# The third batch's q turned by VectorE instead of TensorE, with the order's positions chosen anew, in a linear-attention and softplus kernel

## The chip, the cores and the metric

The kernel runs on one core of a Trainium2 chip. The time is the device time in microseconds of one execution. Before the change it is 912.41 us, the median of three runs (911.59 to 914.95).

A core has engines that each work through a queue of their own, in order: TensorE (PE, matmuls; its weight loads are shown apart as PEld), VectorE (DVE), ScalarE (ACT), GpSimd (POOL) and SyncE (SP), which here only issues transfers between DRAM and on-chip memory. Sixteen DMA engines carry the transfers. Engines wait for each other through semaphores.

## The reference

Shapes: q, k, v are 8 batches x 8 heads x 576 rows x 64; x becomes 4608 tokens x 512; w_in is 512 x 2048 and w_out 2048 x 512.

```python
kv  = np.einsum('bhsd,bhse->bhde', k, v)
out = np.einsum('bhsd,bhde->bhse', q, kv)
rms = np.sqrt(np.mean(out * out, axis=-1, keepdims=True) + 1e-06)
x   = (out / rms * g_norm)            # then (B,H,S,D) -> (B*S, H*D)
h   = x @ w_in
g   = np.maximum(h, 0.0) + np.log1p(np.exp(-np.abs(h)))
y   = g @ w_out
```

## The kernel before, in words

**Three factors.** Each fp32 operand of the two large products is split into three parts (`high`, `low`, `less`), so that `h = x @ w_in` takes 12 matmuls per step (L660) and each of the three token tiles of a step takes 3 matmuls of `g @ w_out` (L667).

**Blocks, chunks and steps.** Tokens are cut into 36 tiles of 128 rows; three tiles make a block (384 tokens, 12 blocks). The inner width of 2048 is cut into 16 chunks of 128. A step is one block with one chunk: 192 steps in all. They are ordered in three phases: phase 0 takes every block with its first 4 chunks (blocks 0 to 3) or 6 chunks (the rest), phases 1 and 2 the later chunks. Between the phases the partial sums of a block go to DRAM (`part`) and come back. A step runs L660 on TensorE, softplus (L682) and a first factor (L684) on ScalarE, the two other factors (L671, L675) on VectorE, and then nine L667 on TensorE.

**From q to x.** For each batch `b`, k and v are loaded and multiplied to `kv` (L502). For each tile `t`, `rows(t)` takes q, needs it turned (head dimension on the partitions), multiplies it with `kv` (L521, `out_rows`, into a half of `o_banks`), squares on ScalarE (L590), sums on VectorE (L525), takes the power -0.5 on GpSimd (L528, L529) and scales on VectorE (L533). Tiles 0 to 11 are then turned by TensorE (L539), copied by ScalarE (L599) and stored to DRAM (L600); later tiles are turned in blocks of 32 by VectorE (L616) and stored by four transfers (L620). Each block's x is read back (L638) and split by ScalarE and VectorE (L445, L448, L452); for block 0 and the first pass of block 1 it is split right from TensorE's turn. Tiles of 128 rows do not line up with batches of 576: tile 13 holds 64 rows of batch 2 and 64 of batch 3, and tile 22 and others mix two batches as well.

**Two ways to turn q.** In `rows`, the condition at L548 chooses.

- By tiles: two transfers per tile piece (L567, `halves`, runs of 64 numbers, 256 bytes), then four TensorE transposes (L577) into `tp` or a half of `o_banks`, then a ScalarE copy (L584) into the tile `qT`.
- By batches: `load_q(b)` issues eight transfers (L423) that bring a whole batch's q into the buffer `qa`, in blocks of 32 x 32 that are laid out so that VectorE's block transpose finishes the turn. A transfer has 1152 runs of 32 numbers (128 bytes). Each tile piece is then one VectorE transpose (L552), which writes `qT` directly. Before the change this is used for batches 3 to 7 (`b >= 3`).

There is one `qa` buffer. The first of the eight transfers of a batch takes it and so waits until VectorE has made the last transpose of the batch before. Batch 0's whole tiles use `qa` as well, loaded by tiles.

**What sets the order.** All work is declared as tasks with an engine, a cost in ns, predecessors, buffers from rings (`rings`: 13 of `m`, one `qa`, two of `o`, one `tp`, two of `raw` and so on) and a position. `Plan.order()` walks through them with these costs: on each engine it takes the task that could start first, or, among those within 150 ns of it, the one with the lowest position. Where TensorE would stand idle for 400 ns or more before step 6, it puts in a filler matmul (`warm`, L778). The result is a fixed order for each queue; on the chip every instruction waits for its operands, and nothing overtakes on its engine. SyncE's transfers are one such queue: a store that waits for its data holds the loads behind it.

**Positions.** `P0` (L190) holds 40 numbers: `CONVERT` and `FETCH` place the first eight weight loads and their conversions; `EARLY` places the tiles of x, k and v, q, the reading back of x and of the partial sums; `LATER` places the later weights. In `weight`, the raw words of w_in or w_out are converted on ScalarE and VectorE (L294 to L324) and split (`divide`, L356 to L378).

Of the kernel before, what the change touches and what calls it, by code (L numbers as in the profile page):

```python
# [40 lines left out]
class Plan:  # L41
# [15 lines left out]
    def slot(self, ring):  # L57
        return Slot(ring)

    def add(self, engine, ns, run, after=(), pos=0.0, take=(), give=(), size=0, behind=None, follows=None):  # L60
        t = Task(engine, ns, run, [a for a in after if a is not None], pos, list(take), list(give), size)
        for s in t.give:
            s.readers += 1
        self.tasks.append(t)
        t.follows = follows
        t.behind = behind
        return t
# [79 lines left out]
def kernel(  # L147
# [39 lines left out]
    PLACES = 8  # L187
    LAST = PHASES[-1]

    P0 = [-88.5, 0.8, -46.3, -8.2, -11.1, 2.0, -42.9, 2.7, -64.0, -43.8, -63.7, -16.7, -31.2, -9.7, 0.3,  # L190
          -4.7, 5.0, -33.5, 16.5, 10.5, 5.5, 8.5, -2.0, 2.5, 3.5, 26.0, -22.0, 10.0, 4.5, 41.0, 50.0,
          65.5, 54.5, 72.0, 91.5, 94.5, 114.5, 106.0, 109.5, 8.5]
    CONVERT, FETCH, EARLY, LATER = P0[:8], P0[8:16], P0[16:27], P0[27:]
    BY_PE = 12
    AT_ONCE = 2 * TB
# [29 lines left out]
    def new(s, shape, dtype=F32):  # L225
        if s.ring == "o":
            s.tile = o_banks[:, :, s.place]
            return s.tile
        pool = ps if s.ring in PS else sb
        s.tile = pool.tile(shape, dtype, tag=f"{s.ring}_{s.place}", name=f"{s.ring}_{s.place}")  # L230
        return s.tile

    def pairs(x, p):

        return x[:, 2 * p:2 * p + 2].rearrange("r h d -> r (h d)")


    def halves(src, e):

        return src[e * NP:(e + 1) * NP].rearrange("p s d -> s p d")  # L240
# [155 lines left out]
    def parts(t):  # L396

        b, s0 = divmod(t * P, S)
        if s0 + P <= S:
            return [(b, 0, P, s0)]  # L400
        return [(b, 0, S - s0, s0), (b + 1, S - s0, P - S + s0, 0)]
# [11 lines left out]
    def load_q(b):  # L413


        q_slots[b], q_loads[b] = slot("qa"), []
        pos = x_pos(first_tile[b] + 1) - EARLY[7]

        def run(a, p):
            if not (a or p):  # L420
                new(q_slots[b], [P, NP * S])
            e, c = divmod(a, 2)
            nc.sync.dma_start(  # L423
                out=q_slots[b].tile[BL * a:BL * (a + 1), p * S:(p + 2) * S].rearrange("j (i d) -> j i d", d=BL),
                in_=q[b, e * NP + p:e * NP + p + 2, :, BL * c:BL * (c + 1)].rearrange("p (i j) d -> j (p i) d", j=BL))

        for a in range(4):
            for p in range(0, NP, 2):
                q_loads[b].append(add("SP", 500, lambda a=a, p=p: run(a, p), (), pos + 0.1 * (2 * a + p // 2),
                                      [q_slots[b]] if not (a or p) else [], [], 1095, behind=int(pos) - 3,  # L430
                                      follows=q_loads[b][-1] if a or p else None))
# [76 lines left out]
    def rows(t):  # L508
# [32 lines left out]
        def part_of_qT(n, r0):  # L541
            if qT.tile is None:
                new(qT, [P, NP, P])
            return qT.tile[:, :, r0:r0 + n]

        turned = []
        for b, r0, n, s0 in parts(t):
            if b >= 3:  # L548
                if b not in q_slots:
                    load_q(b)  # L550
                turned.append(add(
                    "DVE", 690 if n == P else 420, lambda b=b, r0=r0, n=n, s0=s0: nc.vector.transpose(  # L552
                        out=part_of_qT(n, r0),
                        in_=q_slots[b].tile.rearrange("k (p s) -> k p s", p=NP)[:, :, s0:s0 + n]),
                    q_loads[b], pos - 1, [qT] if not r0 else [], [q_slots[b]], follows=turned[-1] if turned else None))
                continue

            if 0 not in q_slots:
                q_slots[0] = slot("qa")
            at_qa = n == P and b == 0  # L560
            q_s = q_slots[0] if at_qa else slot("m")

            def load(b=b, n=n, s0=s0, q_s=q_s, at_qa=at_qa):
                if q_s.tile is None:
                    new(q_s, [P, NP * S] if at_qa else [P, H, D])
                for e in range(2):
                    nc.sync.dma_start(out=natural(q_s, at_qa)[:n, e::2], in_=halves(q[b, :, s0:s0 + n], e))  # L567

            def natural(q_s, at_qa):
                if not at_qa:  # L570
                    return q_s.tile
                return q_s.tile[:, t * d_model:(t + 1) * d_model].rearrange("s (h d) -> s h d", d=D)

            def turn_q(n=n, q_s=q_s, at_qa=at_qa, tp=slot("tp" if t < AT_ONCE else "o")):
                y = new(tp, [P, NP, P])
                for p in range(NP):
                    nc.tensor.transpose(y[:, p, :n], pairs(natural(q_s, at_qa)[:n], p), ident[:n, :n])  # L577

            tp = turn_q.__defaults__[-1]
            ld = add("SP", 900, load, (), pos - EARLY[7], [q_s] if not at_qa or t == 0 else [], [], 1220 * n // P,  # L580
                     behind=int(pos) - 3, follows=first_load[0] if t and at_qa else None)
            first_load.append(ld)
            a = add("PE", 440, turn_q, [ld], pos - 1, [tp], [q_s])
            turned.append(add("ACT", 590, lambda n=n, r0=r0, tp=tp: nc.scalar.copy(part_of_qT(n, r0), tp.tile[:, :, :n]),  # L584
                              [a], pos - 1, [qT] if not r0 else [], [tp], follows=turned[-1] if turned else None))
# [172 lines left out]
    for b in range(B):  # L758
        kv_of(b)
        for t in range(n_tiles):  # L760
            if parts(t)[-1][0] == b:
                rows(t)
# [51 lines left out]
```

## Time and profile before

| What | Value |
|---|---|
| Median of three runs | 912.41 us (911.59 to 914.95) |
| The profiled execution: time | 912.41 us |
| The profiled execution: span, first to last instruction | 910.6 us |
| TensorE clock granted, mean | 0.996 |
| Idle time of TensorE ahead of L660, ahead of L667 | 0.2 us, 0.0 us |
| Turns of q by VectorE (L552) | 20 of 688 ns and 5 of 430 ns |
| Turns of q by TensorE (L577) from `m` or `qa` | 60 transposes in all |
| Transfers of q: L423 | 40 of 144 KB, 4.9 us from issue to landing (median) |
| Transfers of q: L567 | 30 of 64 or 128 KB |
| Moved by DMA | 131.59 MB, mean 144 GB/s |

How the lines are read: a group of instructions gives line, engine, operation, what it writes `<-` what it reads, its shapes, `xcount`, then the busy time and the mean ns of one, then how long the engine stood idle ahead of it and what ended that. A timeline gives start and length in us, then the same names; in brackets stands the idle time ahead and its releaser. A stretch gives its length, then each engine's busy time with the count of instructions, the granted clock, the DMA engines' mean busy share and GB/s. Matmuls overlap, so the lengths of neighbours on TensorE's timeline do not add up; their starts do.

### The profile page before, as it was taken

How to read it: one execution, taken by the hardware profiler on the slowest of the kernel's cores; microseconds unless marked ns; L12 is line 12 of the kernel's file. 1: busy time of each engine (PE TensorE's matmuls, PEld its weight loads, DVE VectorE, ACT ScalarE, POOL GpSimd, SP SyncE). 2: the span in 40 equal slices, each digit the busy share in tenths (PEclk: the TensorE clock that was granted, in tenths of full speed). 3: DMA queues.
4: the chain of work that ended last, by engine and by line, in shares of the span. 5: the costliest groups of instructions: out<-in, count | busy, mean ns of one | idle time of the engine just before them, and what ended most of it. 6: DMA issues, size and time to landing. Idle time of an engine off the chain costs nothing.

```text
span 910.6 us, 15638 instructions
## 1 busy us (share of the span) xinstructions
PE 898.8 (99%) x6005; PEld 791.6 (87%) x6005; DVE 621.7 (68%) x1049; ACT 411.4 (45%) x793; POOL 86.6 (10%) x79
## 2 busy tenths in 40 slices
PE   7999999999999999999999999999999999999998
PEld 5687788888888889999999899999999899999987
DVE  6887888575567886888668787886444555555553
ACT  4776555434343555644434544554323333333331
POOL 0444222132113200000000000000000000000000
PEclk8999999999999999999999999999999999999999
DMA  9999867959581636355344445541330433433323
GB/s 254 258 254 245 227 171 207 178 133 191 162 175 38 168 103 185 105 168 179 104 127 128 150 139 176 201 166 37 104 97 8 139 104 87 122 104 105 104 70 104
DMA packets 207259, 131.59 MB, mean 144 GB/s; under 512 B 98128, under 2 KB 181072, under 8 KB 207184
## 3 DMA queue, kind: packets, MB, share of 16 engines
q1 hardware_dynamic: 207024, 130.59, 52.3%
q8 instruction: 47, 0.77, 0.4%
q14 instruction: 28, 0.23, 0.1%
q10 hardware_dynamic: 160, 0.00, 0.0%
HBM read 91.75 MB, written 38.80 MB: 143 GB/s over the span
## 4 chain that ended last, share of the span: by engine, by line
PE 96%; DMA 2%; ACT 1%; issue 0%; DVE 0%; SPq 0%; DVEq 0%
PE h L660 45%; PE s L667 44%; PE o_banks L521 2%; DMA m<-in_v_dram 2%; PE tp L502 2%; PE h L778 1%; PE s L502 1%; PE o_banks L577 0%; PE o_banks L539 0%; ACT x L590 0%; PE h L374 0%; ACT m L584 0%; PE tp L539 0%; ACT m L599 0%; PE h L375 0%
## 5 line engine op out<-in xcount | busy, mean ns | idle before, releaser
L660 PE MATMUL h<-xv,w 128*128 128x384 f32 x2304 | 435.1, 337 | 0.2 <-ACT w L378 0.2
L667 PE MATMUL s<-w,gv 128*128 128x512 f32 x1728 | 434.3, 395 | 0.0
L660 PEld LDWEIGHTS h<-xv,w 128*128 128x128 f32 x2304 | 406.2, 188 | 16.0 <-ACT w L378 0.4
L667 PEld LDWEIGHTS s<-w,gv 128*128 128x128 f32 x1728 | 319.4, 188 | 61.2 <-DVE gv L675 0.2
L682 ACT ACTIVATE g<-h 128x384 f32<-128x384 f32 x192 | 94.3, 491 | 396.8 <-PE h L660 389.7
L671 DVE TENSOR_TENSOR gv<-g,gv 128x384 fp32r<-128x384 f32 x192 | 106.5, 555 | 191.6 <-ACT gv L684 190.8
L684 ACT ACTIVATE gv<-g 128x384 fp32r<-128x384 f32 x192 | 100.8, 525 | 23.9 <-PE s L667 16.6
L675 DVE SCALAR_TENSOR_TENSOR gv<-gv 128x384 fp32r<-128x384 f32 x192 | 106.8, 556 | 5.8
L448 DVE SCALAR_TENSOR_TENSOR xv<-m,g_col,xv 128x512 fp32r<-128x512 f32 x102 | 75.9, 744 | 2.9 <-ACT xv L445 2.9
L452 DVE SCALAR_TENSOR_TENSOR xv<-xv 128x512 fp32r<-128x512 f32 x108 | 74.4, 689 | 2.6
L445 ACT ACTIVATE xv<-m,g_down 128x512 fp32r<-128x512 f32 x102 | 70.2, 711 | 5.6 <-DMA m<-x 5.5
L529 POOL TENSOR_TENSOR r<-r,half 128x8 f32<-128x8 f32 x36 | 68.3, 1896 | 3.0
L709 DVE SCALAR_TENSOR_TENSOR m<-s,scale,m 128x512 f32<-128x512 f32 x24 | 17.9, 746 | 29.7 <-PE s L667 29.7
L528 POOL TENSOR_SCALAR r<-r 128x8 f32<-128x8 f32 x36 | 16.9, 470 | 219.0 <-DVE r L525 218.7
L533 DVE TENSOR_TENSOR x<-o_banks,r 128x512 f32<-128x512 f32 x36 | 24.7, 687 | 12.9 <-PE o_banks L521 5.1
L709 DVE SCALAR_TENSOR_TENSOR m<-s,m 128x512 f32<-128x512 f32 x36 | 23.7, 685 | 9.0 <-PE s L667 9.0
L311 ACT ACTIVATE sq<-sq,big 128x512 bf16<-128x512 bf16 x32 | 22.9, 716 | 12.4 <-DVE m L307 12.4
L359 DVE TENSOR_TENSOR m<-m,w 128x512 f32<-128x512 f32 x30 | 20.6, 687 | 11.6 <-ACT w L356 11.5
L521 PEld LDWEIGHTS o_banks<-kv,m 64*64 64x64 f32 x1152 | 20.1, 134 | 8.9 <-issue 5.3
L525 DVE TENSOR_REDUCE r<-x 128x8 f32<-128x512 f32 x36 | 24.4, 679 | 3.8 <-ACT x L590 3.7
L590 ACT ACTIVATE x<-o_banks 128x512 f32<-128x512 f32 x36 | 21.4, 594 | 9.3 <-DVE x L533 4.5
L521 PE MATMUL o_banks<-kv,m 64*64 64x64 f32 x1152 | 25.0, 224 | 0.6 <-ACT m L584 0.5
(71 smaller groups left out, 436.0 us busy)
## 6 DMA issues: line engine op xcount, KB each, us to landing
m<-x SPq DMA_DIRECT2D x102, 256.0 KB, 4.5
part<-m SPq DMA_DIRECT2D x72, 256.0 KB, 2.3
m<-part SPq DMA_DIRECT2D x72, 256.0 KB, 4.0
raw<-in_moe_w_in_dram SPq DMA_DIRECT2D x16, 512.0 KB, 5.6
m<-in_k_dram SPq DMA_DIRECT2D x32, 256.0 KB, 5.4
m<-in_v_dram SPq DMA_DIRECT2D x32, 256.0 KB, 5.1
raw<-in_moe_w_out_dram SPq DMA_DIRECT2D x16, 512.0 KB, 5.8
qa<-in_q_dram SPq DMA_DIRECT2D x40, 144.0 KB, 4.9
```

What stands on the lines that cost most here:

```text
L445: nc.scalar.activation(cols(0, F32R), x.tile, func=AF.Identity, scale=g_down)
L448: nc.vector.scalar_tensor_tensor(out=cols(1, F32R), in0=x.tile, scalar=g_col, in1=cols(0), op0=ALU.mult, op1=ALU.subtract)
L452: nc.vector.scalar_tensor_tensor(out=cols(2, F32R), in0=cols(1), scalar=-RADIX, in1=cols(0), op0=ALU.mult, op1=ALU.add)
L521: nc.tensor.matmul(y[r0:r0 + P // 2, a, c0:c0 + D], lhsT=qT.tile[e * D:(e + 1) * D, p, r0:r0 + P // 2], rhs=kvs[b % 2][e * D:(e + 1) * D, ...
L529: nc.gpsimd.tensor_tensor(out=r.tile, in0=r.tile, in1=half, op=ALU.pow)
L660: nc.tensor.matmul(hp, lhsT=w_in.tile[:, i, kd * P:(kd + 1) * P], rhs=xv.tile[:, i, kd], start=(m == 0), stop=(m == 3 * KD - 1))
L667: nc.tensor.matmul(mine[i].tile, lhsT=gv.tile[:, m, i * P:(i + 1) * P], rhs=w_out.tile[:, m], start=(c == cs[0] and m == 0), stop=(c == cs ...
L671: nc.vector.tensor_tensor(out=gv.tile[:, 1], in0=g.tile, in1=gv.tile.bitcast(F32)[:, 0], op=ALU.subtract)
L675: nc.vector.scalar_tensor_tensor(out=gv.tile[:, 2], in0=f32[:, 1], scalar=-RADIX, in1=f32[:, 0], op0=ALU.mult, op1=ALU.add)
L682: a = add("ACT", 490, lambda: nc.scalar.activation(new(g, [P, NT]), h.tile, func=AF.Softplus, scale=1.0 + E), [a], s, [g], [h])
L684: a = add("ACT", 530, lambda: nc.scalar.activation(new(gv, [P, 3, NT], F32R)[:, 0], g.tile, func=AF.Copy, scale=DOWN), [a], s, [gv])
L709: a = add("DVE", 700, lambda: nc.vector.scalar_tensor_tensor(out=new(ot, [P, d_model]), in0=bank.tile, scalar=(scale if ph == LAST else 1. ...
```

## The change

The condition in `rows` moves from `b >= 3` to `b >= 2`: batch 2, the third, now comes by `load_q` and is turned by VectorE. It covers tiles 9 to 12 and the first half of tile 13. Ten L567 transfers, five turns by TensorE (20 transposes) and five ScalarE copies go; eight L423 transfers and five VectorE transposes come. The cutting of a batch into eight transfers of 1152 runs is the same function in both programs. Most positions in `P0` have new values, so that the order of every queue is planned again. Nothing else differs.

```diff
-    P0 = [-88.5, 0.8, -46.3, -8.2, -11.1, 2.0, -42.9, 2.7, -64.0, -43.8, -63.7, -16.7, -31.2, -9.7, 0.3,
-          -4.7, 5.0, -33.5, 16.5, 10.5, 5.5, 8.5, -2.0, 2.5, 3.5, 26.0, -22.0, 10.0, 4.5, 41.0, 50.0,
-          65.5, 54.5, 72.0, 91.5, 94.5, 114.5, 106.0, 109.5, 8.5]
+    P0 = [-72.5, -3.2, -24.8, -9.7, -19.6, 1.5, -23.9, 2.2, -63.0, -49.3, -55.7, -21.2, -38.7, -7.7,
+          -2.7, -4.7, 2.0, -26.5, 14.0, 10.5, 5.5, 17.5, -2.0, 2.5, 3.5, 21.5, -35.0, 10.0, 6.5, 41.0,
+          51.0, 65.5, 53.5, 72.5, 90.5, 95.5, 114.5, 109.5, 111.5, 8.5]
...
         for b, r0, n, s0 in parts(t):
-            if b >= 3:
+            if b >= 2:
                 if b not in q_slots:
                     load_q(b)
                 turned.append(add(
```

## The prediction

> **What bounds the kernel now.** I read the page first (busy times, slices), then the busy times by stretch, then TensorE's, VectorE's and SyncE's timelines around the tiles that the change touches. The page:
>
> ```profile
> PE 898.8 (99%) x6005; PEld 791.6 (87%) x6005; DVE 621.7 (68%) x1049; ACT 411.4 (45%) x793; POOL 86.6 (10%) x79
> ...
> DMA  9999867959581636355344445541330433433323
> ...
> L667 PE MATMUL s<-w,gv 128*128 128x512 f32 x1728 | 434.3, 395 | 0.0
> ```
>
> TensorE is busy for 99% of the span. The two main matmul groups hardly ever wait, so a microsecond taken from TensorE's own work counts in full, if nothing else becomes late. The DMA engines are full only in the first slices. Stretches of 8 us (columns: length, then busy time of PE, PEld, DVE, ACT, POOL, granted clock, DMA share, GB/s):
>
> ```profile
> 72.00:80.00 8.00, 7.69 (x81) 5.91 (x77) 6.06 (x12) 5.45 (x12) 3.59 (x4) 1.00 1.04 219
> 80.00:88.00 8.00, 7.90 (x125) 6.57 (x125) 5.47 (x9) 5.72 (x11) 3.77 (x3) 1.00 0.90 257
> 88.00:96.00 8.00, 7.58 (x72) 6.18 (x71) 6.39 (x12) 4.52 (x9) 2.75 (x4) 1.00 0.73 195
> 96.00:104.00 8.00, 8.00 (x122) 6.24 (x121) 6.24 (x11) 3.76 (x8) 3.01 (x3) 1.00 0.98 264
> ```
>
> Here, where the third batch (b = 2) is attended to, TensorE idles 0.31 + 0.10 + 0.42 us, DMA is full until 80 us and again from 96, and VectorE works 75% of the time. From 100 us on, TensorE is busy for 20.00 of every 20 us. The turns to be removed, on TensorE's timeline:
>
> ```profile
> 71.05 0.66 PE L577 MATMUL o_banks<-ident_r,m 128*128 128x128 f32 x4 [0.21 <-ACT m L599]
> ...
> 72.83 0.60 PE L577 MATMUL o_banks<-ident_r,m 128*128 128x128 f32 x4
> 73.18 2.33 PE L660 MATMUL h<-xv,w 128*128 128x384 f32 x12
> ...
> 77.98 0.66 PE L577 MATMUL o_banks<-ident_r,m 128*128 128x128 f32 x4 [0.31 <-ACT x L590]
> 78.39 1.65 PE L667 MATMUL s<-w,gv 128*128 128x512 f32 x6
> ```
>
> Matmuls overlap, so the cost of a turn is from its start to the next start: 72.83 to 73.18 is 0.35, not 0.60. The L660 at 73.18 is step 4, the first of block 1.
>
> **The change part by part.** The profiled execution took 912.41 us with a span of 910.6, 1.8 us lying around it; it is also the median of the three runs, so the sum is made against 912.41 directly. The order of the two programs' instructions is the same for TensorE's first 77 rows (to step 0's first matmuls, 42.5 us) and SyncE's first 41, so the start is costed at nothing: everything that could hide or expose it is unchanged.
>
> *TensorE, removed.* Five turns (four full, one half): start to next start 0.59 (71.05), 0.35 (72.83), 0.41 (77.98), 0.35 (90.27) and 0.39 (94.83), sum 2.09. Filler matmuls (L778) fall from 55 to 54, and one costs 0.32 (four took 1.29). Together −2.41. The waits just ahead of three of these turns (0.21, 0.31, 0.32) may go too: the gain is at most 3.25. ScalarE loses five copies (4 × 0.589 + 0.374 = 2.73 us); at 4.5 to 5.7 of 8 us it is not the limit, so I take nothing for it, though it can shorten waits that end in an ACT row.
>
> *VectorE, added.* Five transposes: 4 × 0.69 + 0.43 = 3.19 us, on an engine that runs in order. Two stand directly ahead of the split (L448, L452) of block 1's last tile. In the trace that split starts at 70.06 after a wait of 0.78 and ends near 71.5, so 1.65 us before step 4 needs it. With two turns and a filler gone (0.59 + 0.35 + 0.32, and the wait of 0.21), TensorE would be at step 4 at 71.7; by TensorE's own rows the last x turn (L539) ends near 68, and the chain behind it is reduce 0.69, two transposes 1.38, L359 0.69, L448 0.75, L452 0.69, so about 72.7 with semaphores, matmuls at 72.9. **Step 4: +1.2 back**, bounds 0 and 1.4 (the two transposes whole).
>
> *Tile 13, the new wait.* The buffer `qa` exists once. Tile 13 needs the end of batch 2 and the start of batch 3. Before, only batch 3 came through `qa`, from 48.7 us on. Now batch 2's eight loads take those places, and batch 3's first load waits until VectorE has turned batch 2's last piece. What VectorE waited for before, between 72 and 100 us (brackets):
>
> ```profile
> 74.75 0.69 DVE L533 TENSOR_TENSOR x<-o_banks,r 128x512 f32<-128x512 f32 x1 [0.30 <-POOL r L529]
> ...
> 77.96 0.69 DVE L525 TENSOR_REDUCE r<-x 128x8 f32<-128x512 f32 x1 [1.20 <-ACT x L590]
> ...
> 86.27 0.69 DVE L533 TENSOR_TENSOR x<-o_banks,r 128x512 f32<-128x512 f32 x1 [1.74 <-PE o_banks L521]
> ```
>
> All such waits there are 0.30 + 1.20 + 0.21 + 0.78 + 1.74 + 0.99 + 0.55 = 5.8 us. After step 4's split the changed order puts 40 instructions on VectorE up to tile 13's second part and tile 14: six L533, five L525, nine halves of a gv split (0.556 each), three pairs L448/L452, six weight rows, L359, L366, one L616 and the remaining transposes; at the groups' means 25.4 us. TensorE reaches tile 13 at 101.4: before it came there at 100.54; the new order has one more L660 set and one more L667 triple done by then (2.2 + 0.7), less 2.41 and 0.84, plus step 4's 1.2. From 72.9 that is 28.5 us. If the 5.8 us of waits recur, VectorE needs 31.2 and TensorE waits 2.7; if half are absorbed, nothing. I take **+2.7**, since the makers of these waits (square, POOL root, product) are all still there.
>
> The load itself: batch 3's last five transfers stand on SyncE behind the store of tile 10's x. That needs tile 10's product, TensorE's turn and a copy, by my chain about 88.3. Prices:
>
> ```profile
> 59.78 2.75 SPq L567 DMA_DIRECT2D m<-in_q_dram  x4
> ...
> 74.18 3.54 SPq L423 DMA_DIRECT2D qa<-in_q_dram  x3
> ...
> 129.16 7.57 SPq L423 DMA_DIRECT2D qa<-in_q_dram  x8
> ```
>
> One `qa` transfer takes 0.95 (7.57/8) to 1.18 (3.54/3). The last is issued near 92 to 93 and lands 4.9 (median) to 7.6 (longest) later: 97 to 100.6. With 1.1 for two transposes that is in time or just late. The bound comes from DMA: of 80 to 96 us only 0.10 × 8 + 0.27 × 8 = 3.0 us were free, seven more `qa` transfers cost 6.7 to 8.2, and before 80 us some 4 are relieved; backlog at most 4.5. Bounds of the whole wait: 0 and 7.1. Behind VectorE's transpose stand step 7's and step 8's gv splits, so their L667 would be late with it.
>
> The Trainium skill, page "DMA: Bandwidth & Descriptors", section "Why small descriptors are slow (HBM only)", speaks against this change: a fixed 3 cycles per packet beside one per 32 bytes. Pieces of 128 bytes instead of 256 would make a batch of q dearer by 14/11, 1.27. By that estimate, and 6.51 us for the ten tile loads, a batch would take 8.3 us; batch 3's seven transfers 7.2 and the sum below would stay as it is. The rows say 7.57 (129.16) to 9.40 (211.54) against 6.51 (2.75 + 1.33 + 1.03 + 1.40), so 1.16 to 1.44.
>
> *Tile 22.* Five transfers of batch 5 move behind block 4's part stores and the x loads that ran from 177.46 to 180.74. Five issues at 0.95 to 1.18 and a landing of 4.9 to 7.6 give 189 to 193 for the data; TensorE needs it two steps later than before (after step 26's L660, 187.80 in the old trace), about 192. I take 0, bounds 0 and 1.5.
>
> *The other positions.* Later weights, x loads and part loads are reordered. Counted in steps, each split of x ends two or three steps ahead of its use in both orders. Chunk 4's w_out loses one step of lead (1.5 to 0.5), chunk 15's w_in three (5 to 2). The cover is TensorE's own backlog with DMA at 0.3 to 0.5; 0, and if it failed once, up to one step's 2.1 us.
>
> **Sum:** 912.4 − 2.4 + 1.2 + 2.7 = 913.9. Ends: 909.2 (−3.25 and no wait) and 912.4 − 2.4 + 1.4 + 7.1 + 1.5 + 2.1 = 922.1.
>
> **The rivals.**
> *Slower: tile 13's q is late because of DMA.* For it: a DMA share of 0.98 to 1.04 around the gap, one buffer, a store ahead of five loads on the same queue. Against: in the old trace batch 3's last transfer was issued at 84 and its transpose ran at 89.89 without a wait. Price 7.1: 912.4 − 2.4 + 1.2 + 7.1 = 918.3. It decides (over +0.5%, 4.6 us) once the wait passes 5.8 us, so when VectorE starts that transpose after some 107 us.
>
> *Faster: everything stays covered.* For it: no TensorE wait after 100 us before; ScalarE is relieved, and it ended VectorE's longest reduce wait. Against: VectorE's 25.4 of 28.5 us. It gives 909.2 to 910.0. More than 0.5% faster (below 907.8) would need 1.4 us beyond every removed row and wait.
>
> *The change does less than its words.* Both programs cut q into eight transfers a batch, at the same line; no piece gets smaller that was already on this path. Then only the third batch and the order count, as costed.
>
> **How the numbers follow.** Tell-apart bound: 0.5%, 4.6 us. Forecast (waits of 1 to 5 us eat the gain): 0.44, 911 to 916. DMA rival or a larger knock-on of it: 0.42, 916 to 922. Covered: 0.14, with a third of it below 907.8 for waits I can't see. So faster 0.05, slower 0.42, the rest within 0.5%. The range leaves out the lowest of the covered case and what is above both bounds: 909.5 to 922.
>
> **What would show it.** Right: 54 fillers, five L577 fewer; step 4 at 72.5 to 73.5; a TensorE wait of 1 to 5 us at an L521 near 101 us, its data from VectorE's L552; no wait later. DMA rival: that L552 waits for `qa` from in_q_dram. Covered: no such wait, TensorE 2 to 3 us earlier from 110 us on. Wrong: a wait of TensorE over 1 us in a place not named, or before 42 us.

## The result, and the profile after

The changed kernel takes 908.94 us (median of four runs, 908.24 to 909.06), the kernel before 912.33 us (four runs, 911.59 to 914.95) on the same chip. The ratio is 0.9956, 95% interval 0.9936 to 0.9976: 3.4 us faster. The prediction said 913.9 and a range of 909.5 to 922.0, so the time lies 0.6 us below its lower end. The profiled execution took 908.87 us with a span of 907.1 us, against 912.41 and 910.6 us.

The page of the changed kernel, the lines that answer to those shown of before:

```profile
PE 894.2 (99%) x5984; PEld 789.1 (87%) x5984; DVE 624.6 (69%) x1054; ACT 409.9 (45%) x788; POOL 82.8 (9%) x79
...
DMA  9999988579672626355344446550330433433323
...
L667 PE MATMUL s<-w,gv 128*128 128x512 f32 x1728 | 433.9, 395 | 0.0
```

TensorE loses 4.6 us of busy time and stays at 99%; VectorE gains 2.9. The stretches around the third batch (same columns as in the prediction):

```profile
72.00:80.00 8.00, 8.00 (x112) 6.41 (x112) 6.53 (x12) 4.32 (x9) 1.96 (x3) 1.00 1.15 320
80.00:88.00 8.00, 8.00 (x126) 6.70 (x125) 6.82 (x13) 4.98 (x10) 4.30 (x4) 1.00 1.05 285
88.00:96.00 8.00, 7.69 (x76) 6.69 (x69) 5.84 (x10) 4.51 (x8) 4.65 (x4) 1.00 0.96 144
96.00:104.00 8.00, 8.00 (x99) 6.94 (x98) 7.03 (x13) 5.67 (x11) 0.31 (x2) 1.00 0.93 277
```

TensorE idles 0.31 us in these 32 us, where it idled 0.83 before, although DMA is now full from 72 to 88 us and VectorE is at 82% instead of 75%. TensorE's timeline at the places the prediction named, and at a late load of v (66.43):

```profile
66.43 0.69 PE L502 MATMUL tp<-m,m 128*64 128x64 f32 x16 [0.94 <-DMA m<-in_v_dram]
...
71.06 0.40 PE L778 MATMUL h<-ident_r 128*128 128x512 f32 x1
71.87 0.69 PE L502 MATMUL tp<-m,m 128*64 128x64 f32 x16 [0.42 <-DVE xv L448]
...
73.06 2.25 PE L660 MATMUL h<-xv,w 128*128 128x384 f32 x12
...
98.80 2.24 PE L667 MATMUL s<-w,gv 128*128 128x512 f32 x9
100.97 1.16 PE L521 MATMUL o_banks<-kv,m 64*64 64x64 f32 x64
102.06 2.34 PE L667 MATMUL s<-w,gv 128*128 128x512 f32 x9
```

The L660 at 73.06 is step 4, 0.13 us earlier than before. The L521 at 100.97 is tile 13; its 64 matmuls are those of tile 13 and then of tile 14, and its bracket is missing, so there is no wait. VectorE's timeline shows how that came about:

```profile
71.06 0.75 DVE L448 SCALAR_TENSOR_TENSOR xv<-tp,g_col,xv 128x512 fp32r<-128x512 f32 x1 [0.49 <-ACT m L599]
...
72.46 0.68 DVE L533 TENSOR_TENSOR x<-o_banks,r 128x512 f32<-128x512 f32 x1
73.06 0.68 DVE L525 TENSOR_REDUCE r<-x 128x8 f32<-128x512 f32 x1
73.66 0.70 DVE L552 STREAM_TRANSPOSE m<-qa 128x512 f32<-128x512 f32 x1
74.28 0.52 DVE L671 TENSOR_TENSOR gv<-g,gv 128x384 fp32r<-128x384 f32 x1
...
79.17 0.69 DVE L525 TENSOR_REDUCE r<-x 128x8 f32<-128x512 f32 x1 [0.94 <-ACT x L590]
...
100.04 1.03 DVE L552 STREAM_TRANSPOSE m<-qa 128x256 f32<-128x256 f32 x2
```

The three instructions from 72.46 on last 0.68 to 0.70 us and start 0.60 us apart. The last line is two transposes, without a wait for their load. By the trace's single records the short one, tile 13's second half, ends at 100.47, half a us before TensorE reaches tile 13; the other, tile 14's, ends at 101.07, and TensorE reaches tile 14 at 101.49. SyncE had issued that load in time:

```profile
89.17 4.23 SPq L423 DMA_DIRECT2D qa<-in_q_dram  x5
```

**Where the time went.** The starts of the L660 sets give the gain by place. At step 0 the new kernel is 0.64 us ahead, with the same order of TensorE's instructions up to there; the changed kernel and those below that differ from it only after step 0 had that step anywhere between 39.1 and 42.0 us, so this part is no more than chance. At step 4 it is 0.13 us ahead, from step 34 on 3.47, at the end 3.55. So the saving arises between steps 4 and 34. There, TensorE's time by line, each matmul counted from its start to the next start:

| Steps 4 to 34 | before | after | difference |
|---|---|---|---|
| Turns of q (L577) | 1.16 | 0 | -1.16 |
| L660, 360 in both | 65.81 | 64.93 | -0.88 |
| L667, 270 in both | 66.61 | 65.55 | -1.06 |
| Idle | 0.83 | 0.31 | -0.51 |
| L521, L502 | 23.00 | 22.63 | -0.37 |
| Turns of x (L539), 16 and 20 | 1.94 | 2.58 | +0.64 |
| Sum | 159.35 | 156.00 | -3.35 |

Over the whole program L577 falls from 6.35 to 3.92 us, and the fillers from 55 to 54. The surprise is that 1.94 us lies in main matmuls (L660 and L667) whose number did not change.

### The profile page after: what moved, and what is told of

It is laid out like the page before. It is cut to its first block, busy times and chain, and to the rows that moved or that the text cites. A ratio compares the mean times of both kernels' runs of the same rounds, so it can differ in the third digit from the quotient of the medians.

```text
span 907.1 us, 15612 instructions
## 1 busy us (share of the span) xinstructions
PE 894.2 (99%) x5984; PEld 789.1 (87%) x5984; DVE 624.6 (69%) x1054; ACT 409.9 (45%) x788; POOL 82.8 (9%) x79
## 4 chain that ended last, share of the span: by engine, by line
PE 95%; DMA 3%; ACT 1%; DVE 0%; issue 0%; SPq 0%
PE h L660 44%; PE s L667 44%; DMA m<-in_v_dram 2%; PE o_banks L521 2%; PE tp L502 2%; PE h L778 1%; PE s L502 1%; PE tp L577 0%; DMA x<-m 0%; ACT m L599 0%; DVE xv L448 0%; PE tp L539 0%; PE o_banks L539 0%; PE h L374 0%; ACT m L584 0%
## 5 line engine op out<-in xcount | busy, mean ns | idle before, releaser
L660 PE MATMUL h<-xv,w 128*128 128x384 f32 x2304 | 434.8, 337 | 0.2 <-ACT w L378 0.2
L667 PE MATMUL s<-w,gv 128*128 128x512 f32 x1728 | 433.9, 395 | 0.0
L660 PEld LDWEIGHTS h<-xv,w 128*128 128x128 f32 x2304 | 406.4, 188 | 16.4 <-ACT w L378 0.7
L667 PEld LDWEIGHTS s<-w,gv 128*128 128x128 f32 x1728 | 319.6, 188 | 60.8 <-DVE gv L675 0.2
L671 DVE TENSOR_TENSOR gv<-g,gv 128x384 fp32r<-128x384 f32 x192 | 106.5, 555 | 174.5 <-ACT gv L684 173.7
L448 DVE SCALAR_TENSOR_TENSOR xv<-m,g_col,xv 128x512 fp32r<-128x512 f32 x102 | 75.9, 744 | 0.6 <-ACT xv L445 0.6
L529 POOL TENSOR_TENSOR r<-r,half 128x8 f32<-128x8 f32 x36 | 65.3, 1813 | 3.0
L533 DVE TENSOR_TENSOR x<-o_banks,r 128x512 f32<-128x512 f32 x36 | 24.8, 688 | 15.3 <-POOL r L529 10.1
L521 PEld LDWEIGHTS o_banks<-kv,m 64*64 64x64 f32 x1152 | 19.9, 134 | 10.7 <-issue 4.7
L525 DVE TENSOR_REDUCE r<-x 128x8 f32<-128x512 f32 x36 | 24.3, 679 | 5.0 <-ACT x L590 4.7
L521 PE MATMUL o_banks<-kv,m 64*64 64x64 f32 x1152 | 24.6, 224 | 1.2 <-ACT m L584 0.7
L590 ACT ACTIVATE x<-o_banks 128x512 f32<-128x512 f32 x36 | 21.2, 594 | 7.6 <-PE o_banks L521 3.9
```

The source lines that it names most:

```text
L448: nc.vector.scalar_tensor_tensor(out=cols(1, F32R), in0=x.tile, scalar=g_col, in1=cols(0), op0=ALU.mult, op1=ALU.subtract)
L521: nc.tensor.matmul(y[r0:r0 + P // 2, a, c0:c0 + D], lhsT=qT.tile[e * D:(e + 1) * D, p, r0:r0 + P // 2], rhs=kvs[b % 2][e * D:(e + 1) * D, ...
L529: nc.gpsimd.tensor_tensor(out=r.tile, in0=r.tile, in1=half, op=ALU.pow)
L660: nc.tensor.matmul(hp, lhsT=w_in.tile[:, i, kd * P:(kd + 1) * P], rhs=xv.tile[:, i, kd], start=(m == 0), stop=(m == 3 * KD - 1))
L667: nc.tensor.matmul(mine[i].tile, lhsT=gv.tile[:, m, i * P:(i + 1) * P], rhs=w_out.tile[:, m], start=(c == cs[0] and m == 0), stop=(c == cs ...
L671: nc.vector.tensor_tensor(out=gv.tile[:, 1], in0=g.tile, in1=gv.tile.bitcast(F32)[:, 0], op=ALU.subtract)
```

## The experiments

**The two halves of the change, alone.** The positions of the changed kernel with the old route:

```diff
-            if b >= 2:
+            if b >= 3:
```

> The kernel before with the new positions alone: batch 2 still comes by tiles and is turned by TensorE. Theory A, the route gives the gain (five turns off TensorE, 2.4 us by their rows, and main sets less often broken up, 1.7 us): about 912.0 to 913.5, since TensorE has all its turns again and only 53 fillers instead of 55 (-0.6). Rival B, the new positions give the gain: 908.5 to 909.5, as the changed kernel.

Measured 915.48 us (913.84 to 917.20), before 913.04; ratio 1.0024 (1.0013 to 1.0035): slower than both expectations. And the new route with the positions of before:

```diff
-            if b >= 3:
+            if b >= 2:
```

> The kernel before with the new condition alone (b >= 2), positions unchanged. Theory A: the five turns are gone, 908.5 to 910, a microsecond or two more where the positions do not fit. Rival B: 912 or more, for without the new positions VectorE's transposes and the eight transfers come at the wrong places.

Measured 909.63 us (908.48 to 911.41); ratio 0.9962 (0.9950 to 0.9975). The route gives the whole gain. The new positions alone cost 2.4 us on the old route, and with the new one they make no difference that these intervals can tell. In the trace with positions alone TensorE idles 10.2 us in all, against 6.4 in the trace before. Two of the waits (line, what it waited for, us in total, times, longest):

```profile
PE tp L502 <- DMA m<-in_v_dram: 1.9, 2, 1.6
...
PE o_banks L539 <- ACT m L584: 1.3, 1, 1.3
```

The second is ScalarE's copy of a turned q (L584), which the new route does without.

**VectorE's margin.** The changed kernel, with each transpose of batch 2 made twice:

```diff
-                    "DVE", 690 if n == P else 420, lambda b=b, r0=r0, n=n, s0=s0: nc.vector.transpose(
+                    "DVE", 690 if n == P else 420, lambda b=b, r0=r0, n=n, s0=s0: [nc.vector.transpose(
...
-                        in_=q_slots[b].tile.rearrange("k (p s) -> k p s", p=NP)[:, :, s0:s0 + n]),
+                        in_=q_slots[b].tile.rearrange("k (p s) -> k p s", p=NP)[:, :, s0:s0 + n])
+                        for _ in range(2 if b == 2 else 1)],
```

> The changed kernel with each VectorE transpose of batch 2 made twice, in the same order of work: 3.2 us more on VectorE between 68 and 80 us. The transposes ahead of step 4 (2 of them, start to start 0.6 each) delay its split by 1.2 us, which TensorE can not hide, if step 4 is bound by VectorE as forecast: about 910. If VectorE has room there and later (it stood idle 4.5 us between step 4 and tile 13), 908.9 to 909.3. If VectorE is at its limit up to tile 13: 911.5 to 912.

Measured 909.39 us (909.12 to 910.08); ratio 0.9960 (0.9948 to 0.9973). In the trace, taking its start (0.52 us later) as zero, the kernel is 0.27 us early at step 4 and 0.65 late from step 5 on, and keeps that. TensorE waits 1.05 us for L448 ahead of step 4, instead of 0.42, and 0.87 us for L533 behind it. But the trace of the changed kernel had lost 0.94 us there to a late load of v, and this one did not. Three executions below whose program is the same up to step 80 and whose v came in time need 188.4 to 188.6 us from step 0 to step 34; this one needs 190.0. So 3.2 us more of VectorE instructions cost some 1.5 us of the trace, and none of it at tile 13; the median moves by 0.45. The same for batch 3, whose first transposes are those that tiles 13 and 14 need (`b == 3` in the last line of the diff):

> The changed kernel with each VectorE transpose of batch 3 made twice. The first two (tile 13's second part and tile 14) stand right ahead of TensorE's L521 at 101 us: 0.36 + 0.60 more there. If VectorE was just in time for tile 13, TensorE waits 0.9 to 1.0 and the time is 909.8 to 910. If there was room of a microsecond or more: 908.9 to 909.2.

Measured 909.36 us (908.00 to 912.55); ratio 0.9966 (0.9954 to 0.9979). Here the delay is in one place. Between step 8 and step 9 the trace loses 0.90 us:

```profile
103.74 0.72 PE L521 MATMUL o_banks<-kv,m 64*64 64x64 f32 x32
105.11 0.69 PE L521 MATMUL o_banks<-kv,m 64*64 64x64 f32 x32 [0.65 <-DVE m L552]
```

The first row is tile 13, still without a wait; the second is tile 14, which waits for its doubled transpose. So the changed kernel has little to spare here: the two transposes end 0.5 and 0.4 us before TensorE needs them, and 1.2 us more on VectorE is a wait. The median hides this (it moves by 0.4 us): the start varied by more, and step 0 of this profiled execution came 2.4 us later.

**The load as the bound.** In the changed kernel each transfer of batch 3 is followed by a copy of the same pieces to memory that nothing reads:

```diff
+            if b == 3:
+                spare = spares[a, p]
+                nc.sync.dma_start(
+                    out=spare.rearrange("j (i d) -> j i d", d=BL),
+                    in_=q[b, e * NP + p:e * NP + p + 2, :, BL * c:BL * (c + 1)].rearrange("p (i j) d -> j (p i) d", j=BL))
```

> The changed kernel with each of batch 3's eight q transfers followed on the same queue by a copy of the same pieces into an unused DRAM tile: twice the traffic and the issues around that load, nothing else. The last q transfer is issued 4 to 8 us later. DMA rival (that load is near the limit): TensorE waits 2 to 7 us at tile 13, 911 to 916. If the load had room of 5 us or more: 908.9 to 910.

Measured 912.68 us (909.03 to 914.72); ratio 0.9998 (0.9985 to 1.0012). VectorE's and TensorE's timelines:

```profile
103.91 1.04 DVE L558 STREAM_TRANSPOSE m<-qa 128x256 f32<-128x256 f32 x2 [2.18 <-DMA qa<-in_q_dram]
```

```profile
104.41 1.29 PE L527 MATMUL o_banks<-kv,m 64*64 64x64 f32 x62 [1.50 <-DVE m L558]
```

(L558 and L527 are L552 and L521, moved by the added lines.) The last load is issued at 100.47 instead of 92.55, the transpose waits 2.18 us for it, and the trace loses 1.95 us between steps 8 and 9. So the DMA rival's mechanism exists. How far off it was stands in the trace of the changed kernel: the last load landed at 96.91, 3.1 us before its transpose began. The median is 3.7 us above the changed kernel's; step 0 of this profiled execution also came 2.25 us later, ahead of any copy, and whether that is chance is not shown. A second `qa` buffer, the plainest way to take this dependence away, was not tried.

**What a turn costs TensorE.** The kernel before, with the 20 transposes of batch 2 made twice:

```diff
-                for p in range(NP):
+                for p in [p for p in range(NP) for _ in range(2 if b == 2 else 1)]:
```

> The kernel before with each of batch 2's 20 TensorE transposes made twice, same order of work. If such a turn costs TensorE its start-to-start time in full, the five turns' 2.09 us less their pipeline entry, so 1.5 to 2.1 more: 913.8 to 914.4. If the two turns ahead of step 4 (0.94 us) are hidden by VectorE's split there, as the trace after suggests, only three count: 913.1 to 913.5. If all are hidden: 912.3.

Measured 915.24 us (912.98 to 915.99); ratio 1.0022 (1.0014 to 1.0031). That is 2.2 us for 20 transposes; the trace, without its start, gives 2.50, of which 0.34 is a late load of v. A break is a place where other matmuls stand between those of L660 and L667, the main stream. Transposes were then put into the quiet part of the changed kernel, steps 80 to 179, where the order has next to no breaks, one and four behind each L660 set:

```diff
+            if 80 <= s < 180:
+                for p in range(4):
+                    nc.tensor.transpose(o_banks[:, p, 0], ident, ident)
```

> The changed kernel with one extra 128x128 fp32 transpose by TensorE (result unused) behind the L660 set of each of the 100 steps 80 to 179, where TensorE never waits. If a foreign instruction between main sets costs only its own time (a turn's four took 0.35 us, so 0.09): +9 us, 918. If it also breaks up the main sets, as their 2.28 against 2.09 us start to start suggest (+0.19): +28 us, 937.

> The same with four transposes at each of the 100 places, a whole turn. Own time alone: +35 us, 944. With one break a place: +54 us, 963. The difference to the run with one transpose gives the price of a transpose (26 us by the rows: 3 x 100 x 0.087), and what is left of that run is the break.

Measured 920.47 us (919.42 to 921.61), ratio 1.0084 (1.0066 to 1.0102), and 952.56 us (952.14 to 953.20), ratio 1.0433 (1.0416 to 1.0451). The steps 80 to 180 of the traces grow by 0.123 and 0.445 us a step. So a transpose of 128 x 128 costs 0.107 us (a third of the difference), and the break itself 0.015: my theory of dear breaks fell for them. The timeline with four:

```profile
501.52 2.27 PE L660 MATMUL h<-xv,w 128*128 128x384 f32 x12
503.63 0.60 PE L664 MATMUL o_banks<-ident_r 128*128 128x128 f32 x4
503.98 2.33 PE L670 MATMUL s<-w,gv 128*128 128x512 f32 x9
506.15 2.27 PE L660 MATMUL h<-xv,w 128*128 128x384 f32 x12
```

A turn takes 0.35 us in its own row (503.63 to 503.98), and the L667 set behind it (here L670) takes 2.17 instead of 2.08. The whole is 0.445: the last transpose of a group has only 0.03 us to the next start, and the rest of its 0.107 shows in the first L667, which takes 0.32 instead of 0.23. So a reading from start to next start misses 0.09 us of a turn.

**Are positions or the route the cause?** Forty positions were searched anew with the planner's own costs, once for the new route and once for the old:

```diff
+    P0 = [-66.5, 0.0, -70.5, -13.0, -23.0, 1.5, -93.5, 3.0, -71.0, -66.5, -48.5, -33.5, -43.0, -10.5,
+          -0.5, -30.5, 4.0, -33.0, 17.0, 10.0, 6.5, 16.5, -1.5, 2.5, 3.5, 109.0, -21.5, 10.0,
+          6.5, 36.0, 50.0, 68.5, 54.5, 72.5, 85.0, 89.5, 116.0, 105.5, 110.5, 8.5]
```

> Question: does the gain of the new route stay when the order's positions are chosen anew for it, in the same manner as for the old route? This kernel is the changed one (third batch by VectorE, b >= 2) with a third set of 40 positions, found by a search over the kernel's own planner; e11 is the old route (b >= 3) with a set found by the same search. Theory (the route's five turns of TensorE are worth about 2.2 us start to start wherever the order puts the rest, and the positions add or take 1 to 3 us each way): this kernel at 906 to 909 us, and e11 1.5 to 3 us above it. Rival (the gain belongs to the match of route and positions, and a well placed old route is as fast): both within 1 us of each other, near 907 to 909 us.

```diff
+    P0 = [-96.0, 0.5, -76.0, -1.0, -3.0, -10.0, -16.5, 1.5, -126.0, -71.0, -72.5, -24.5, -42.0, -14.5,
...
             if b >= 3:
```

> The old route (third batch turned by TensorE, b >= 3) with positions found for it by the same search. Theory: 908 to 911 us, that is 1.5 to 3 us above e10, and 2 to 4 us below the kernel before if the planner's end of the order (4 us earlier) carries over to the chip. Rival: within 1 us of e10.

New route 906.90 us (906.23 to 908.38), ratio 0.9938 (0.9926 to 0.9949); old route 911.19 us (910.25 to 914.57), ratio 0.9985 (0.9974 to 0.9996). The new route with these positions has the lowest median of all kernels here. The old route stays 4.3 us above it, more than the 1.5 to 3 expected: of the traces' difference of 3.9 us, 2.16 are the turns and 1.89 are waits; the other lines cancel. The route was worth 3.4 us with the old positions, some 6.5 with the new ones (915.48 against 908.94, from two sessions; by the ratios 6.2), and 4.3 with positions searched for each route. A batch more by VectorE, positions searched in the same way:

```diff
-            if b >= 2:
+            if b >= 1:
```

> One size changed: a batch more by VectorE (b >= 1, batches 1 to 7), with positions found by the same search as for e10 and e11 (their planned ends were 897.1 for e10's, 897.2 for e11's, 900.6 us for this one). Theory (turns leave TensorE, 2.2 to 2.4 us a batch, but batch 1 is needed while the DMA engines are full and VectorE splits the first weights, so the saved work comes back as fillers and waits before step 6): 909 to 913 us, so 2 to 6 us above e10, with more fillers than e10 and the first steps later. Rival (each batch that is moved yields what the third did): 902 to 905 us.

Measured 908.68 us (908.45 to 909.37); ratio 0.9959 (0.9945 to 0.9972). Against the kernel of 906.90 us TensorE's turns fall by 2.14 us more and its fillers rise by 2.96 (47 to 56): by this account batch 1's turns stood where TensorE had no main matmuls to do.

**What breaks the main stream.** Left open was the 1.94 us in L660 and L667. Quarter-size matmuls (64 x 64, the form of L521; L502 is 128 x 64) were put into steps 80 to 179, four in one place:

```diff
+            if 80 <= s < 180:
+                for e, half in ((0, 0), (1, 1), (0, 1), (1, 0)):
+                    nc.tensor.matmul(o_banks[half * 64:half * 64 + 64, 2 * e, 0, :D], lhsT=ident[e * D:(e + 1) * D, half * 64:half * 64 + 64],
+                                     rhs=ident[e * D:(e + 1) * D, :D], start=True, stop=True)
```

> The changed kernel with four quarter-size matmuls (64 x 64 x 64, the form of L521 and L502) behind the L660 set of each of steps 80 to 179, written to a buffer that is free by then. The profile accounts give the saving that I can't place: between step 4 and step 34 the same 360 L660 and 270 L667 take 1.94 us less in the new order, and the new order breaks their stream 28 times where the old one broke it 36 times. In both traces an L660 ahead of such a break starts its successor 0.27 us later instead of 0.17, and one behind it 0.28. Theory (a break by quarter-size matmuls costs some 0.2 us in its neighbours, beyond its own matmuls at 0.039 each): 0.155 + 0.20 = 0.35 a step, so near 944 us. Rival (a break costs nearly nothing, as with the transposes): 0.155 + 0.015 = 0.17 a step, near 926 us.

Two and two, the second pair behind the last L667 of the step:

```diff
+            if 80 <= s < 180:
+                for e, half in ((0, 0), (1, 1)):
...
+            if 80 <= s < 180 and i == TB - 1:
+                for e, half in ((0, 1), (1, 0)):
```

> The same 400 matmuls, but two behind the L660 set and two behind the L667 sets of each step, so twice as many breaks. Theory: 100 more breaks at 0.2 us, so 20 us (15 to 25) above the kernel with one place. Rival: 1.5 us above it.

And the four transposes split in the same way:

```diff
+            if 80 <= s < 180:
+                for p in (0, 1):
+                    nc.tensor.transpose(o_banks[:, p, 0], ident, ident)
...
+            if 80 <= s < 180 and i == TB - 1:
+                for p in (2, 3):
+                    nc.tensor.transpose(o_banks[:, p, 0], ident, ident)
```

> The four 128 x 128 transposes of the kernel with four breaks (952.56 us), but two behind the L660 set and two behind the L667 sets of each step. Theory (the dear break belongs to the change between whole and quarter-size matmuls, and transposes of 128 x 128 are whole): 100 more breaks at about 0.015 us, so 952 to 956 us. Rival (every break of the main stream costs 0.2): 972 us.

Quarters in one place 955.27 us (954.29 to 956.77), ratio 1.0469 (1.0443 to 1.0495); in two places 998.68 us (998.57 to 1001.47), ratio 1.0953 (1.0919 to 1.0987); transposes in two places 951.15 us (950.75 to 952.63), ratio 1.0425 (1.0400 to 1.0451). A hundred more breaks by the same quarter-size matmuls cost 43 us, 0.43 each; a hundred more by transposes cost nothing. The timeline with two places:

```profile
501.88 2.36 PE L660 MATMUL h<-xv,w 128*128 128x384 f32 x12
504.17 0.33 PE L664 MATMUL o_banks<-ident_r 64*64 64x64 f32 x4
504.43 2.33 PE L671 MATMUL s<-w,gv 128*128 128x512 f32 x9
506.69 0.33 PE L675 MATMUL o_banks<-ident_r 64*64 64x64 f32 x4
506.95 2.38 PE L660 MATMUL h<-xv,w 128*128 128x384 f32 x12
```

The L660 set lasts 2.29 us from start to start (501.88 to 504.17) instead of 2.09, the L667 set 2.26 instead of 2.08, and a pair of quarters 0.26. Within the sets the excess is at the ends: the last L660 ahead of a break takes 0.268 instead of 0.175, the first behind one 0.281. So about 0.2 us of a break is paid by its neighbours and the rest by the quarters themselves, which take 0.26 to 0.28 us a group whether there are two or four. The neighbours of the kernel's own groups show the same figures in the trace before: L660 ahead of L502 or L521 0.268, behind them 0.281; L667 0.32 and 0.337 instead of 0.231.

With these figures the 1.94 us can be placed. In both traces of steps 4 to 34 an undisturbed L660 takes 0.174 us and an undisturbed L667 0.231, so what was saved stands in the main matmuls next to a break. Next to breaks with L502 or L521 the excess was 6.5 us in 32 breaks and is 5.3 us in 27. Next to breaks of transposes alone it was 0.7 us in four, three of them turns of batch 2, and is 0.1 us in one. About 0.1 us more stands at the first L660 of step 4. The number of breaks goes with the route: over the whole program L502 or L521 break the main stream 51 times before and with the new positions alone, 47 times after and with the new route alone.

**Fewer breaks.** If breaks cost that much, an order with fewer of them should gain. The planner gets a cost for the break and prefers to stay with the kind of matmul that it is at; positions searched with it:

```diff
+    QUARTERS, BREAK, STAY = (600, 640), 430, 4
...
-                            key=lambda o: (o[1].pos, o[0]))
+                            key=lambda o: (o[1].pos - self.STAY * (engine == "PE" and (o[1].ns in self.QUARTERS) == quarter), o[0]))
...
+            if t.engine == "PE":
+                if t.ns in self.QUARTERS and not quarter:
+                    engine_free["PE"] += self.BREAK
+                quarter = t.ns in self.QUARTERS
```

> The new route (b >= 2), and the planner now knows the break: it adds 430 ns to TensorE where a quarter-size group (L502, L521) follows whole ones, and among tasks that could start within 150 ns it prefers to stay with the kind it is at; positions searched with that cost. TensorE's order then changes 34 times from whole to quarter-size groups instead of 65 in the changed kernel and 61 in the kernel with the third set of positions (906.90 us). Theory (a break costs 0.43 us on the chip in this order too): 27 to 31 breaks fewer are 12 to 13 us; part of them stood where TensorE waited anyway and some loads are wanted sooner, so 895 to 901 us. Rival (most breaks are hidden where they stand, in the stretches with fillers and waits): 905 to 908 us.

> The same with the positions of another search: 31 breaks, planned end 0.9 us later. Theory: within 3 us of the kernel with 34 breaks, 895 to 902 us. Rival: 905 to 909 us.

Measured 908.78 us (907.86 to 912.84), ratio 0.9965 (0.9952 to 0.9978), and 908.48 us (907.26 to 911.46), ratio 0.9962 (0.9948 to 0.9975). Neither came near the 895 to 902 us of the theory. The account of the order with 31 breaks against the one with 61 (906.90 us) says where the saving went: L660 falls by 2.15 us and L667 by 3.11, together 0.175 for each break that went, which is the neighbours' part and no more; the fillers fall by 3.0 us, and TensorE's idle time rises from 7.8 to 14.5 us. (These two profiled executions took 907.26 and 908.38 us, so they are not in the order of the medians.) The largest group of its waits (columns: line, what it waited for, us in total, times, longest; L526 and L595 are L521 and L590, moved by the added lines):

```profile
PE o_banks L526 <- ACT x L595: 4.2, 7, 0.7
```

Where `out_rows` of several tiles stand together, the next one finds `o_banks` not yet free and waits, by the profile for ScalarE's square; in the other orders main matmuls stood between. So a break costs this kernel's main matmuls 0.18 to 0.2 us, not 0.43 (the rest was the added quarters' own), and what its removal saves came back as waits.

## Why the prediction was wrong

**Tile 13, +2.7: the step that failed.** No wait came. The instructions were counted rightly: 40, whose lengths sum to 25.4 us in the trace as forecast. Three things were off. Their lengths overlap, by 1.86 us in all: I had seen that TensorE's starts and not lengths add up, and did not apply it to VectorE, though the trace before has 1.46 us of overlap between 72 and 100 us. The waits between them were 5.0 us instead of 5.8 (4.5 us of those that a bracket shows). And the chain began at 72.46 instead of 72.9. Together 3.1 us, and the data came at 101.07 instead of 104.1. It was near: with each transpose of batch 3 doubled, tile 14 waited and the trace lost 0.9 us.

**TensorE, removed: right in size.** The five turns were put at 2.09 us; the rows of L577 fell by 2.43, and doubling these turns cost 2.2. One filler went, as said. What a start-to-start reading misses is 0.09 us a turn, in the main matmul behind it.

**Step 4, +1.2: the time is right, the reason is not.** TensorE was forecast there at 72.9, within 72.5 to 73.5, and came at 73.06. But VectorE's two added transposes did not hold it up. In VectorE's row at 71.06 above, the split's L448 starts after 0.49 us in which VectorE was idle, by the profile until a copy of ScalarE (L599). TensorE had lost 0.94 us to the late load of v (at 66.43), which the prediction did not have, and it lost 0.42 us more at the L502 that waits for L448 (at 71.87). In four executions of the experiments with the same program up to there (one transpose, transposes in two places, quarters in two places, batch 3's load doubled) v came in time. Steps 0 to 4 then took 32.4 to 32.6 us instead of 33.4; the trace before has 32.9. VectorE was idle for 0.5 to 1.4 us ahead of L448, and TensorE's wait was 0.41 us all the same. One of them:

```profile
69.61 0.75 DVE L448 SCALAR_TENSOR_TENSOR xv<-tp,g_col,xv 128x512 fp32r<-128x512 f32 x1 [1.43 <-ACT m L599]
```

So the match of 73.06 with 72.9 is luck. VectorE sets the time there only with the transposes doubled, where L448 follows without idle time and TensorE waits 1.05 us.

**The load: right.** Forecast issue of the last transfer 92 to 93 us, measured from 92.55 to 93.40; it landed at 96.91, within the forecast 97 to 100.6 but for 0.1 us, and the transpose did not wait. The DMA rival (chance 0.42) was too likely: the load had 3.1 us to spare.

**Tile 22, 0: right.** The L521 of that tile shows no wait.

**The other positions, 0: no late load in steady work, but a term of TensorE left out.** The bound was one late load of up to 2.1 us; the late v ahead of step 4 was one of 0.94. What I put at nothing without a reason is what the order does to the main matmuls. Between steps 4 and 34 their stream is interrupted 28 times instead of 36, and they take 1.94 us less: 1.2 next to the breaks with L502 or L521, five fewer, 0.6 next to those of transposes alone, three fewer, and 0.1 at step 4.

**The sum.** With tile 13's wait at its true 0, the prediction's terms give 911.2, and that is still 2.3 us too long. The trace has the rest, each against what the prediction said: start of step 0, -0.64 (chance); steps 0 to 4, +0.57 (with the late v in it); main matmuls between steps 4 and 34, -1.94; waits that went, -0.51; L521 and L502, -0.37; one more turn of x behind step 4, +0.64; small terms, -0.1. That is the 908.9 of the profiled execution. The rival that happened is "everything stays covered", given 0.14; its own times of 909.2 to 910.0 lack the term of the main matmuls too. The range ended at 909.5 because that case was cut off there.

## What to carry to other kernels

Add up starts, not lengths, on every engine that works through a queue, VectorE as well as TensorE. Where one engine is busy for 99%, a small operation moved off it is worth its own row plus what it does to its neighbours: read the first and last main matmul next to it too, and count how often the main stream is interrupted and by which shape; but before merging interruptions, look for the engine that they give time to. A term that rests on 25 us of work against 28 us of time decides the sign of a forecast of 3 us, and deserves its pitch from the trace.

## What the runs showed of the hardware

- VectorE's instructions of 128 x 512 in the rows above last 0.68 to 0.70 us and start 0.60 apart. The Trainium skill, page "VectorE: DVE Perf Modes", section "The DRAIN you can't avoid", lets the next operation start only when the pipe is empty, and sooner where nothing holds it. The trace shows the second: L525 at 73.06, L552 at 73.66 and L671 at 74.28 are three different operations, and each starts 0.08 us ahead of its forerunner's end.
- A transpose of 128 x 128 in fp32 costs TensorE 0.107 us in the busy stream of steps 80 to 179, in one place or two; its own duration is 0.27. The same page's section "Rules for kernel authors" advises TensorE for a 128 x 128 transpose whose result may go to PSUM. In this kernel, with TensorE busy for 99%, the route over VectorE was 3.4 to some 6.5 us faster. It is not the same operation: VectorE turns within blocks of 32 x 32, and the transfers bring the blocks to their places.
- Two or four 64 x 64 matmuls between whole ones cost 0.26 to 0.28 us of their own, and 0.1 us at the last whole matmul ahead and 0.1 at the first behind. With transposes of 128 x 128 in the same place the last matmul ahead costs no more, and the 0.09 at the first behind is what the last transpose's row lacks.
- With one and the same order up to step 0, that step began between 39.1 and 42.0 us in the profiled executions. How much of the spread between runs of one kernel comes from there is not shown: one execution of each was profiled.
